# A feed-forward planner that knows the port, the transfer queue and the measured durations, and three more seven-product steps

## The chip, the cores and the metric

The kernel runs on one core of a Trainium2 chip. The core has a matrix engine (TensorE, PE in the profile), a vector engine (VectorE, DVE), a scalar engine (ScalarE, ACT), GpSimd (POOL) and a queue for transfers (SyncE, SP). The engines run side by side, each takes its own instructions in a fixed order, and they wait for each other by semaphores. The time is the device time of one execution in microseconds (us), lower is better. A difference of about 0.5% is what a measurement of this kernel can tell from no change.

## The reference

Two branches over the same 2048 rows `x` of width 576 are mixed by a gate. Branch A is linear attention with 32 heads of 18 columns. Branch B is a layer norm, a matrix `w1` to 4608 columns, a GELU, and a matrix `w2` back to 576 columns.

```python
def _A_ref(x, wqkv, wo):
    q, k, v = ...                                  # x @ wqkv, 32 heads of 18
    phi = lambda t: jnp.where(t > 0, t + 1, jnp.exp(t)) + 1e-6
    pq, pk = phi(q), phi(k)
    kv = jnp.einsum("bhsd,bhse->bhde", pk, v)
    z = jnp.einsum("bhsd->bhd", pk)
    num = jnp.einsum("bhqd,bhde->bhqe", pq, kv)
    den = jnp.einsum("bhqd,bhd->bhq", pq, z)[..., None] + 1e-6
    o = num / den                                  # the heads side by side again
    return o @ wo

def _B_ref(x, w1, b1, w2, b2):
    y = _layernorm(x, axis=-1)
    h = _gelu(jnp.einsum("bsd,df->bsf", y, w1) + b1)
    return jnp.einsum("bsf,fd->bsd", h, w2) + b2

g = _sigmoid((x * gate_w).sum(-1, keepdims=True))
return g * a + (1 - g) * b
...
```

## The kernel before

Branch A, the gate and the layer norm's sums fill the first 275 us, branch B's feed-forward the rest. This text is about the feed-forward, which begins where the tiles `wa`, `wb`, `h` and `region` appear.

**Numbers in two halves.** Every float32 factor is split into a high part (a copy into the type fp32r, made by ScalarE) and a low part (what is left, a subtraction by VectorE), and a product is taken as high x high, high x low and low x high. The tiles in the order listings are: `u` (the hidden values in float32), `h` (their two parts), `fresh` (raw `w1` and `w2` as they land, and sums of them), `wa` and `wb` (the split `w1`), `region` (the split `w2`), `accs` (the sums of the result in SBUF, and in its spare part the rows of `y`), `ystage` (split pieces of `y` on their way to memory), `ps` (PSUM, where the matmuls write).

**Steps.** The 4608 hidden columns are cut into 18 chunks of 256, the 2048 rows into two halves of 1024. A step `k` is one chunk for one half of the rows: steps 0 to 17 are the first half, 18 to 35 the second. In each step the `w1` product is made by Strassen's scheme in its Winograd form, two blocks by two blocks, with seven products (`up_product`) of seven 512-column matmuls each. The `w2` product of a step is made in the step after it, in one of two ways (`make_units`):

- plain: 8 units of 12 matmuls of 288 columns, 96 in all (`plain_unit`). Of the 8 evictions, those in `SEEDS` start from the running sum, which ScalarE copies into PSUM and back out; the others are added by VectorE (`accs<-ps,accs`).
- seven products: 14 units of 6 matmuls, 84 in all (`one_of_seven`), if `k` is in `SEVEN` (line 64). It needs four sums of blocks of `h` (`make_sum`, S1, S3, S2, S4 in that order, each `u<-u` and then split into `h`), four sums of blocks of `w2` (`sum_w2`, on GpSimd, `fresh<-fresh 128x288`), and it makes 12 evictions on VectorE.

The first half has work that the second has not: the four sums of `w1` (`sum_w1`, on GpSimd, `fresh<-fresh 128x384`), its split (`wa`, `wb`) and store, and the making of the second half's `y`. Before the change, `SEVEN` holds the odd steps of the first half up to 15 and all of 17 to 34, 26 steps, and all sums of `h` stand on GpSimd (`SUM_ENGINE`, line 74).

**The order.** No instruction of the feed-forward stands where the code lists it. `op` and `dma` record each operation with what it needs and gives; `nominal` gives due times by the matmuls' order; then a list planner (`choose`, `commit`) walks all engines by `COST`, a price for each engine as (fixed, per column, extra until the result is seen), and writes each engine's instructions in the order found. `port=True` marks operations with two inputs in SBUF: `when_` (line 1404) lets such an operation of VectorE or GpSimd begin, in the plan, from 135 ns before the end of the other engine's last such operation. Buffers (`h` 9, `u` 5, `w2` 7 places) are handed out by the plan too.

## Time and profile before

| what | value |
|---|---|
| median of 3 runs | 1116.88 us (1116.56 to 1120.96) |
| profiled execution, own time | 1116.29 us |
| its span, first to last instruction | 1114.6 us |
| granted TensorE clock over the span | 1.000 |
| PE / DVE / ACT / POOL busy, share of the span | 99% / 80% / 58% / 36% |

A row of busy time tells how long an engine had something in it. Matmuls overlap, and an end of one is modelled, so that a PE of 99% may still lose time; it is better read by how many matmuls of each width fall into a stretch. The table by stage (`us from the span's start`) cuts the span at 275 us, where the feed-forward begins, at 700 us, about where the second half of the rows begins, and at 1075 us, ahead of the end.

### The profile page before, as it was taken

What the parts mean: (1) busy time and instruction counts of PE and PEld (TensorE: products, weight loads), DVE (VectorE), ACT (ScalarE), POOL (GpSimd) and SP (SyncE); (2) the same over time, 40 slices, a digit from 0 to 9 for tenths busy, and PEclk for the clock granted to TensorE, in tenths of its full rate; (3) what the DMA queues carried; (4) which work ended last, traced back from release to release, by engine and by line L of the source; (5) the groups of instructions that cost most, each with busy time, mean ns of one, the idle gap of its engine ahead of it and who ended that gap; (6) DMA issues with size and microseconds to landing.
All of it is one profiled execution on the core that took longest, in us unless ns stands there. A gap on an engine that the chain in (4) does not pass through costs nothing.

```text
span 1114.6 us, 18587 instructions
## 1 busy us (share of the span) xinstructions
PE 1102.9 (99%) x6766; PEld 1004.2 (90%) x6766; DVE 890.6 (80%) x1381; ACT 647.6 (58%) x1158; POOL 398.2 (36%) x326
## 2 busy tenths in 40 slices
PE   9999999999999999999999999999999999999998
PEld 8999999999888898897898988889989899988998
DVE  4568784895887979879979997888887788778888
ACT  6677774443657566666756766355554555455542
POOL 2111112531335153533515543325444444344430
PEclk9999999999999999999999999999999999999999
DMA  6465762835635646463564649774445444544432
GB/s 183 125 89 184 171 227 102 316 118 210 220 124 181 203 153 233 158 240 129 185 221 157 223 145 380 273 249 122 128 119 147 128 118 127 143 126 125 121 110 86
DMA packets 108862, 189.42 MB, mean 170 GB/s; under 512 B 8924, under 2 KB 68588, under 8 KB 104674
## 3 DMA queue, kind: packets, MB, share of 16 engines
q1 hardware_dynamic: 107858, 187.49, 52.9%
q8 instruction: 53, 0.87, 0.3%
q10 hardware_dynamic: 720, 0.74, 0.2%
q14 instruction: 39, 0.32, 0.1%
q0 software_dynamic: 192, 0.01, 0.0%
HBM read 121.40 MB, written 66.80 MB: 169 GB/s over the span
## 4 chain that ended last, share of the span: by engine, by line
PE 77%; DVE 11%; DMA 5%; ACT 2%; issue 2%; SPq 2%; POOL 1%; ACTq 0%; DVEq 0%; POOLq 0%
PE ps L111 77%; DVE accs L111 3%; DVE h L111 2%; DVE region L111 2%; SPq L111 2%; DMA w1d<-wb 1%; DMA fresh<-in_ue 1%; DVE wb L111 1%; ACT u L111 1%; DVE wa L111 1%; DMA yd<-ystage 1%; DMA accs<-in_xe 1%; DVE u L111 1%; ACT h L111 1%; POOL u L111 0%
## 5 line engine op out<-in xcount | busy, mean ns | idle before, releaser
L111 PEld LDWEIGHTS ps<-region,h 128*128 128x128 f32 x3144 | 454.6, 188 | 43.8 <-DVE accs L111 6.9
L111 PE MATMUL ps<-region,h 128*128 128x288 f32 x3144 | 479.4, 295 | 5.4 <-ACT ps L111 2.0
L111 DVE TENSOR_TENSOR accs<-ps,accs 128x576 f32<-128x576 f32 x336 | 250.7, 754 | 87.8 <-PE ps L111 83.2
L111 POOL TENSOR_TENSOR fresh<-fresh 128x288 f32<-128x288 f32 (+1 forms) x164 | 173.7, 1067 | 372.3 <-DMA fresh<-in_w 281.0
L111 PE MATMUL ps<-y,wa 128*128 128x512 f32 x1008 | 269.0, 393 | 0.4 <-DVE wa L111 0.4
L111 PE MATMUL ps<-y,wb 128*128 128x512 f32 x756 | 203.8, 396 | 0.3 <-ACT u L111 0.3
L111 PEld LDWEIGHTS ps<-y,wa 128*128 128x128 f32 x1008 | 176.6, 188 | 25.6 <-DVE wa L111 1.3
L111 POOL TENSOR_TENSOR u<-u 128x512 f32<-128x512 f32 x104 | 163.7, 1574 | 96.8 <-DVE h L111 60.2
L111 DVE TENSOR_TENSOR h<-u,h 128x512 fp32r<-128x512 f32 x222 | 185.2, 849 | 5.4 <-ACT u L111 4.8
L111 PEld LDWEIGHTS ps<-y,wb 128*128 128x128 f32 x756 | 132.6, 188 | 23.3 <-ACT u L111 0.7
L111 ACT ACTIVATE u<-ps 128x512 f32<-128x512 f32 x73 | 43.7, 598 | 144.8 <-PE ps L111 144.8
L111 PE MATMUL ps<-y 128*128 128x288 f32 (+1 forms) x896 | 126.1, 297 | 1.1 <-ACT y L111 0.5
L111 PEld LDWEIGHTS ps<-y 128*128 128x128 f32 x896 | 122.4, 188 | 3.4 <-ACT y L111 1.3
L111 DVE TENSOR_TENSOR region<-fresh,region 128x576 fp32r<-128x576 f32 x120 | 99.5, 829 | 2.1 <-ACT region L111 1.7
L111 ACT ACTIVATE region<-fresh 128x576 fp32r<-128x576 f32 x120 | 74.1, 630 | 36.5 <-PE ps L111 32.1
L111 ACT ACTIVATE h<-ps,b1s 128x512 fp32r<-128x512 f32 x45 | 30.9, 686 | 77.4 <-PE ps L111 77.2
L111 ACT ACTIVATE h<-u,b1s 128x512 fp32r<-128x512 f32 x73 | 52.7, 721 | 32.1 <-DVE u L111 31.3
L111 ACT ACTIVATE h<-u 128x512 fp32r<-128x512 f32 x104 | 60.3, 621 | 17.3 <-POOL u L111 17.2
L111 DVE TENSOR_TENSOR wa<-fresh,wa 128x512 fp32r<-128x512 f32 x64 | 49.3, 770 | 19.2 <-ACT wa L111 13.8
L111 PE MATMUL ps<-wp,qt 128*128 128x288 f32 x448 | 63.3, 298 | 0.0
L111 DVE TENSOR_TENSOR u<-ps,u 128x512 f32<-128x512 f32 x74 | 50.9, 689 | 13.8 <-ACT u L111 11.7
L111 POOL TENSOR_TENSOR pks<-pks,k 128x576 f32<-128x576 f32 x15 | 21.9, 1459 | 108.7 <-DVE k L111 108.7
(122 smaller groups left out, 1037.9 us busy)
## 6 DMA issues: line engine op xcount, KB each, us to landing
w1d<-wa SPq DMA_DIRECT2D x17, 1280.0 KB
wa<-w1d SPq DMA_DIRECT2D x68, 320.0 KB
fresh<-in_w SPq DMA_DIRECT2D x70, 288.0 KB
y<-yd SPq DMA_DIRECT2D x14, 1280.0 KB
w1d<-wb SPq DMA_DIRECT2D x17, 960.0 KB
wb<-w1d SPq DMA_DIRECT2D x51, 320.0 KB
yd<-ystage SPq DMA_DIRECT2D x28, 320.0 KB
fresh<-in_um SPq DMA_DIRECT2D x64, 128.0 KB
```

Source lines behind the costliest of these rows:

```text
L111: return lambda *args, **kwargs: self.tc.keep_in_program_order(op(*args, **kwargs))
```

## The change

The numbers and names that are new:

- `SEVEN` has 29 steps: 1, 3, 6, 8, 9, 10, 11, 13 to 34. In the first half 11 of the steps 0 to 16 go by seven products (8 before).
- The sums of `h` are divided by `DVE_SUMS`: S1, S3 and S4 of the first half and S1, S3 and S2 of the second stand on VectorE, the others on GpSimd.
- `SEEDS` has three entries for four.
- The planner's prices of VectorE and ScalarE move by 1 ns; GpSimd's go from 30 + 2.5 per column to 250 + 2.19 per column. In the plan, an operation of GpSimd that uses the port begins 78 ns after VectorE's last such operation has ended (before: up to 135 ns ahead of its end), and `in_the_way` puts back an operation whose port time would run into one of the other engine that is due.
- Transfers are planned with their number of issues, a time for what they move, one after another, and no more than eight under way.
- Each GpSimd operation that uses the port gets a semaphore wait for the VectorE operation with the port that stands ahead of it in the plan, if that ended less than 4 us before (`add_manual_dep`).
- `plan` runs first and is written out after; its weights stand in `TUNED`, with an offset to the due time for each kind of operation.
- The last two of eight tiles of attention results for the end (`attn`) lie in `ystage`, not in `fresh`.

```diff
-SEVEN = {*range(1, NCHUNK - 1, 2), *range(NCHUNK - 1, LAST)}
-SEEDS = ((0, 0, 0), (0, 1, 0), (1, 0, 0), (1, 1, 0))
-SUM_ENGINE = {S1: "POOL", S3: "POOL", S2: "POOL", S4: "POOL"}
+SEVEN = set([1, 3, 6, 8, 9, 10, 11, 13, 14, 15, 16, 17, 18, 19, 20, 21, 22, 23, 24, 25, 26, 27, 28, 29, 30, 31, 32, 33, 34])
+DVE_SUMS = set([(2, False), (3, False), (3, True), (4, False), (4, True), (6, True)])
+SEEDS = ((0, 0, 1), (0, 1, 0), (1, 1, 0))
...
-    COST = {ACT: (90, 0.838, 97), DVE: (65, 1.0425, 83), POOL: (30, 2.5, -40)}
+    COST = {ACT: (91, 0.838, 97), DVE: (66, 1.0425, 84), POOL: (250, 2.19, -78)}
...
-        engine = SUM_ENGINE[m]
+        engine = DVE if (m, k < NCHUNK) in DVE_SUMS else POOL
...
-        if o.port:
-            other = POOL if o.engine == DVE else DVE
-            s = max(s, port_until[other] - 135)
...
+            if o.port:
+                s = max(s, port_until[POOL] - 135 if o.engine == DVE else port_until[DVE] + 78)
+            return s
+
+        def in_the_way(o, s):
+            other = POOL if o.engine == DVE else DVE
+            until = min(due[o], s + o.tail - 135 - shift - guard)
+            for u in port_line[other][port_at[other]:]:
+                if due[u] >= until:
+                    return False
+                if u not in done and due[u] + shift > s - 1500 and (missing[u] or ready[u] < s + o.tail - 135):
+                    return True
+            return False
...
+            if e == DMA:
+                service = (o.tail - o.ns - 1800) / o.issues
+                for n in range(o.issues):
+                    if len(landed) >= 8:
+                        s = max(s, landed[-8])
+                    s += o.ns / o.issues
+                    moved = max(moved, s + 600) + service
+                    t = moved + 1200
+                    landed.append(t)
...
+    end, sequence = plan(*TUNED)
+    before = None
+    for o, got, s, t in sequence:
+        for name, key, n in got:
+            places[name, key] = n
         o.f()
+        if o.port and o.engine == DVE:
+            before = dve.last.ins.name, t
+        if o.port and o.engine == POOL and before and before[1] > s - 4000:
+            tc.add_manual_dep(pool.last.ins, before[0], mybir.DependencyInfo(
+                mybir.DependencyClass.Sync, mybir.DependencyReason.DATA), reason="order")
```

Over the whole program the rows of the order count 36 matmuls `ps<-region,h` fewer (of 3140 shown), on DVE 87 sums `u<-u 128x512`, 29 evictions `accs<-ps,accs`, 9 low parts of `h` and 6 of `region` more, on POOL 75 sums `u<-u` fewer and 12 sums of `w2` more, on ACT 34 copies for the seeds fewer and, net, 21 of other kinds more. SP has 613 rows in both. Up to the feed-forward the rows of PE are the same.

On GpSimd, in step 9 (a seven-product step in both kernels), the sums of `w2` and of `h` and those of the next `w1` stood before as follows.

```order
L111 TENSOR_TENSOR fresh<-fresh 128x288 [waits DMAHW7_49,DMAHW6_49]
L111 TENSOR_TENSOR fresh<-fresh 128x288 [waits DVE_49,Activation_49,Pool_49]
L111 TENSOR_TENSOR fresh<-fresh 128x288 [waits Pool_49] x2
L111 TENSOR_TENSOR u<-u 128x512 [waits DVE_49,Activation_49]
L111 TENSOR_TENSOR u<-u 128x512 [waits Activation_49,Pool_49]
L111 TENSOR_TENSOR fresh<-fresh 128x384
L111 TENSOR_TENSOR u<-u 128x512 [waits DVE_49,Pool_49] x2
```

On the same engine, in step 9 of the changed kernel:

```order
L113 TENSOR_TENSOR fresh<-fresh 128x384 [waits DMAHW2_49,DMAHW1_49,DMAHW3_49,DMAHW0_49,DVE_49]
L113 TENSOR_TENSOR fresh<-fresh 128x384 [waits DMAHW4_49,DMAHW5_49,DVE_49,Pool_49]
L113 TENSOR_TENSOR fresh<-fresh 128x384 [waits DVE_49]
L113 TENSOR_TENSOR fresh<-fresh 128x384 [waits DMAHW6_49,DMAHW7_49,DVE_49,Pool_49]
L113 TENSOR_TENSOR fresh<-fresh 128x288 [waits DMAHW6_49,DMAHW5_49,Activation_49]
L113 TENSOR_TENSOR fresh<-fresh 128x288 [waits DVE_49,Pool_49]
L113 TENSOR_TENSOR fresh<-fresh 128x288 [waits Pool_49]
L113 TENSOR_TENSOR fresh<-fresh 128x288 [waits DVE_49,Pool_49]
L113 TENSOR_TENSOR u<-u 128x512 [waits DVE_49,Activation_49]
```

Of the step's four sums of `h` one is left on GpSimd, behind the sums of `w1` and `w2`, and nearly every instruction waits for one of VectorE, also where it needs nothing from it.

On VectorE, the same step before, where the low parts of `h` and `region` and the evictions alternate:

```order
L111 TENSOR_TENSOR accs<-ps,accs 128x2x288 [waits PE_49]
L111 TENSOR_TENSOR region<-fresh,region 128x2x288 [waits DMAHW7_49,DMAHW6_49,Activation_49]
L111 TENSOR_TENSOR u<-ps,u 128x512 [waits PE_49]
L111 TENSOR_TENSOR h<-u,h 128x512
L111 TENSOR_TENSOR h<-u,h 128x512 [waits Activation_49]
L111 TENSOR_TENSOR region<-fresh,region 128x2x288 [waits DVE_49,Pool_49]
L111 TENSOR_TENSOR accs<-ps,accs 128x2x288 [waits PE_49]
L111 TENSOR_TENSOR h<-u,h 128x512 [waits Activation_49,Pool_49]
L111 TENSOR_TENSOR h<-u,h 128x512 [waits Pool_49]
L111 TENSOR_TENSOR region<-fresh,region 128x2x288 [waits DVE_49,Activation_49]
```

And the same step on VectorE after the change:

```order
L113 TENSOR_TENSOR u<-u 128x512
L113 TENSOR_TENSOR accs<-ps,accs 128x2x288 [waits PE_49]
L113 TENSOR_TENSOR accs<-ps,accs 128x2x288
L113 TENSOR_TENSOR region<-fresh,region 128x2x288 [waits Activation_49]
L113 TENSOR_TENSOR h<-u,h 128x512 [waits Activation_49]
L113 TENSOR_TENSOR region<-fresh,region 128x2x288
L113 TENSOR_TENSOR u<-u 128x512 [waits DVE_49,Pool_49]
L113 TENSOR_TENSOR h<-u,h 128x512 [waits Activation_49] x3
L113 TENSOR_TENSOR accs<-ps,accs 128x2x288 [waits PE_49,Activation_49]
L113 TENSOR_TENSOR accs<-ps,accs 128x2x288 [waits PE_49]
```

Two sums `u<-u` stand among the low parts, and the evictions stand in pairs or longer runs.

More of the change, by code (lines that the diff above doesn't have):

```diff
@@ L887, in op @@
             tail = ns + c
-        o = Op(engine, f, ns, tail, needs, gives, port, take, give, by)
-        o.early = early
+        o = Op(engine, f, ns, tail, needs, gives, port, take, give, by, early, issues)
         ops.append(o)
@@ L1089, in there @@
             def there(keys=keys):
[L1090 removed]
+                at = [places["w2", key] for key in keys]
                 if len(at) > 1 and at[0] > at[-1]:
@@ L1109, in start_of @@
     def start_of(k, to, half, first):
-        if k % NCHUNK == 0 and first:
+        if k in (0, NCHUNK) and first:
             return b2b[:, None, half_cols(half)].to_broadcast([P, 2, HALF])
@@ new lines, in tile_gated_mix, with plan, offer, give @@
+    count = {o: sum(key in makers for key in o.needs) for o in ops}
+    in_order, left = [o for o in ops if not count[o]], dict(count)
+    for o in in_order:
+        for u in followers[o]:
+            left[u] -= 1
+            if not left[u]:
+                in_order.append(u)
+    assert len(in_order) == len(ops)
+    def plan(lag, late, slop, slack, guard, ahead):
+        slot, due = {o: n for n, o in enumerate(ups)}, {}
+        for o in downs:
+            _, k, j, n = o.by
+            slot[o] = (k + 1) * SLOTS + lag + j * SLOTS / n
+        t = 0.0
+        for o in sorted(ups + downs, key=lambda o: (slot[o], o.by[0] == "up")):
+            due[o] = t
+            t += o.ns
+        nominal = {o: due[o] for o in due}
+        for o in reversed(in_order):
+            out = [due[u] - o.tail - HEAR.get(u.engine, 0) for u in followers[o]]
+            if o in due:
+                out.append(due[o])
+            due[o] = min(out, default=1e9) - o.early - ahead.get(o.kind, 0)
+        missing, ready = dict(count), {o: 0.0 for o in ops}
+        line = {name: sorted(own, key=lambda o: due[o]) for name, own in lines.items()}
+        at = {name: 0 for name in lines}
+        room = {name: [(0.0, n) for n in range(size)] for name, size in ROOMS.items()}
+        room_of, done, sequence = {}, set(), []
+        free, port_until = {e: 0.0 for e in (PE, ACT, DVE, POOL, DMA)}, {DVE: -1e9, POOL: -1e9}
+        pending = {e: [] for e in free}
+        port_line = {e: sorted((o for o in ops if o.engine == e and o.port), key=lambda o: due[o]) for e in port_until}
+        port_at, moved, landed = {e: 0 for e in port_until}, 0.0, []
+        next_up, next_down, shift = 0, 0, 0.0
+        def offer(o):
+            if o.engine is None:
+                give(o, ready[o])
+            else:
+                pending[o.engine].append(o)
+        def give(o, t):
+            for u in followers[o]:
+                ready[u] = max(ready[u], t + HEAR.get(u.engine, 0))
```

334 lines of the change are left out of this document (143 added, 191 removed).

## The prediction, made before the changed kernel was run

> **What bounds the kernel now.** I read the page's busy shares first, then the table by stage, the waits of the matrix engine, and the timeline around its longest wait.
>
> ```profile
> span 1114.6 us, 18587 instructions
> PE 1102.9 (99%) x6766; PEld 1004.2 (90%) x6766; DVE 890.6 (80%) x1381; ACT 647.6 (58%) x1158; POOL 398.2 (36%) x326
> ```
>
> PE is busy all the time, so what shortens the kernel is fewer matmuls or fewer holes between them. How many holes there are is told by the table by stage, first for all instructions, then for those that touch `region` (on PE, the 288-column matmuls of the `w2` product; the busy columns are then PE, PEld, DVE and ACT alone), and by two rows of PE's timeline.
>
> ```profile
> core 0: us, PE busy (x) PEld busy (x) DVE busy (x) ACT busy (x) POOL busy (x), PEclk, DMA share, GB/s
> 275.00:700.00 425.00, 419.07 (x2464) 373.26 (x2463) 361.94 (x520) 270.16 (x441) 171.84 (x137) 1.00 0.58 199
> 700.00:1075.00 375.00, 375.00 (x2207) 336.71 (x2206) 301.26 (x417) 197.74 (x327) 161.24 (x130) 1.00 0.49 145
> ...
> 275.00:700.00 425.00, 235.39 (x1561) 222.87 (x1562) 51.30 (x54) 32.91 (x54) 1.00 0.58 199
> 700.00:1075.00 375.00, 216.59 (x1394) 205.31 (x1394) 44.70 (x61) 38.72 (x62) 1.00 0.49 145
> ```
>
> ```profile
> 820.61 1.76 PE L111 MATMUL ps<-region,h 128*128 128x288 f32 x12
> 822.20 1.09 PE L111 MATMUL ps<-y,wb 128*128 128x512 f32 x4
> ```
>
> Twelve 288-column matmuls take 822.20 - 820.61 = 1.59 us to the next start, 132.5 ns each. In the second half 1394 of them are 184.7 us; the other 2207 - 1394 = 813 (512 columns) share the 190.3 us left, 234.1 ns each. At this pace the first half's 1561 and 903 would be 206.8 + 211.4 = 418.2 us. They took 425. So the first half has 6.8 us of holes beyond what the second half has, and the clock is 1.00 in both. The waits of PE in the first half say whom it waits for:
>
> ```profile
> PE ps L111 <- ACT ps L111: 2.0, 3, 1.3
> PE ps L111 <- DVE accs L111: 2.0, 5, 0.5
> PE ps L111 <- DVE h L111: 1.0, 2, 0.7
> PE ps L111 <- DVE wa L111: 0.4, 1, 0.4
> PE ps L111 <- ACT u L111: 0.3, 1, 0.3
> ```
>
> The longest is the one of 1.27 us at 506 us, in a seven-product step. GpSimd's, VectorE's and PE's rows ahead of it:
>
> ```profile
> 497.11 3.07 POOL L111 TENSOR_TENSOR u<-u 128x512 f32<-128x512 f32 x2
> 501.58 3.50 POOL L111 TENSOR_TENSOR u<-u 128x512 f32<-128x512 f32 x2
> 505.05 1.44 POOL L111 TENSOR_TENSOR fresh<-fresh 128x384 f32<-128x384 f32 x1
> ```
>
> ```profile
> 497.27 1.76 DVE L111 TENSOR_TENSOR region<-fresh,region 128x576 fp32r<-128x576 f32 x1 [0.89 <-ACT region L111]
> 499.55 1.18 DVE L111 TENSOR_TENSOR h<-u,h 128x512 fp32r<-128x512 f32 x1
> 501.18 0.98 DVE L111 TENSOR_TENSOR h<-u,h 128x512 fp32r<-128x512 f32 x1 [0.45 <-ACT u L111]
> 502.09 1.84 DVE L111 TENSOR_TENSOR region<-fresh,region 128x576 fp32r<-128x576 f32 x1
> 503.85 0.74 DVE L111 TENSOR_TENSOR accs<-ps,accs 128x576 f32<-128x576 f32 x1
> 504.60 2.43 DVE L111 TENSOR_TENSOR h<-u,h 128x512 fp32r<-128x512 f32 x2
> ...
> 506.18 1.85 PE L111 MATMUL ps<-region,h 128*128 128x288 f32 x12 [1.27 <-ACT ps L111]
> ```
>
> While GpSimd sums, VectorE's operations with two inputs in SBUF last 1.0 to 1.8 us; the eviction, which has one input in PSUM, keeps its 0.74. The page's groups for the first half, the durations of single kinds over the feed-forward, and four rows of VectorE at 803 us give the undisturbed prices:
>
> ```profile
> L111 DVE TENSOR_TENSOR h<-u,h 128x512 fp32r<-128x512 f32 x99 | 82.6, 852 | 4.9 <-ACT u L111 4.8
> L111 DVE TENSOR_TENSOR region<-fresh,region 128x576 fp32r<-128x576 f32 x45 | 47.2, 1050 | 2.0 <-ACT region L111 1.7
> L111 DVE TENSOR_TENSOR wa<-fresh,wa 128x512 fp32r<-128x512 f32 x32 | 30.8, 962 | 18.3 <-ACT wa L111 13.8 <-DMA fresh<-in_ue 4.5
> L111 DVE TENSOR_TENSOR wa<-fresh,wa 64x256 fp32r<-64x256 f32 x32 | 18.5, 577 | 0.9
> L111 DVE TENSOR_TENSOR wb<-fresh,wb 128x768 fp32r<-128x768 f32 x16 | 15.2, 951 | 0.1
> ...
> L111 DVE TENSOR_TENSOR h<-u,h x221: 674/683/1780, 286.6 to 1099.4; 128x512 fp32r<-128x512 f32 x111
> L111 DVE TENSOR_TENSOR accs<-accs x32: 550/948/1770, 304.1 to 630.5; 128x768 f32<-128x768 f32 x16, 128x384 f32<-128x384 f32 x16
> L111 DVE TENSOR_TENSOR wa<-accs,wa x4: 422/554/693, 280.1 to 284.2; 128x512 fp32r<-128x512 f32 x2, 64x256 fp32r<-64x256 f32 x2
> ...
> 803.01 0.76 DVE L111 TENSOR_TENSOR accs<-ps,accs 128x576 f32<-128x576 f32 x1
> 803.69 0.68 DVE L111 TENSOR_TENSOR h<-u,h 128x512 fp32r<-128x512 f32 x1
> 804.29 0.75 DVE L111 TENSOR_TENSOR region<-fresh,region 128x576 fp32r<-128x576 f32 x1
> 804.96 0.75 DVE L111 TENSOR_TENSOR accs<-ps,accs 128x576 f32<-128x576 f32 x1
> ```
>
> An operation begins some 0.08 us before the last one's end is shown, so that the price on a full VectorE is the distance of starts: eviction 0.68, low part of `h` 0.60, of `region` 0.67. Against the undisturbed durations (0.68, 0.75, 0.69, 0.42) the first four groups lost 99 x 0.17 + 45 x 0.30 + 32 x 0.27 + 32 x 0.155 = 44 us to waiting for the port.
>
> **The change part by part.**
>
> *Fewer matmuls.* Three steps more by seven products: 3 x (96 - 84) = 36 matmuls x 132.5 ns = 4.8 us off PE. PE is the bound, so all of it counts.
>
> *The holes.* The change moves sums off GpSimd, plans GpSimd's port time at its measured length and makes it wait for VectorE. That aims at the holes of the kind at 506 us: behind ACT `ps`, DVE `accs` and DVE `wa`, 2.0 + 2.0 + 0.4 = 4.4 us. DVE `h` and ACT `u` (1.3 us) I leave: they are late by their own chain. Ends: nothing is gained (0) and all 6.8 us go. I take 4.4.
>
> *VectorE's new work.* A sum on VectorE is in no row. `accs<-accs`, also float32 and from SBUF alone, takes 550 ns for 384 columns and 948 for 768, so 512 lie near 683, or 0.60 from start to start, as `h<-u,h` does. Ends: 0.47 and 0.87 (384 and 768 columns, less 0.08); I take 0.60. Of the 87 sums 11 x 3 = 33 fall into the first half (20 us) and 18 x 3 = 54 into the second (32 us). The 29 evictions (x 0.68), 9 low parts of `h` (x 0.60) and 6 of `region` add 28 us in the first half. A seven-product step of the first half then asks of VectorE 12 x 0.68 + 7 x 0.60 + 3 x 0.60 + (3 x 0.67 + 0.36) for `region` + 3.25 for `wa` and `wb` (2 x 0.61, 2 x 0.34, 0.87, and 0.48 for the 64 rows of `wb`, between 256 and 512 columns) + 2 x 0.60 for `u<-ps,u` = 21.0 us. PE needs 49 x 0.2341 + 84 x 0.1325 = 22.6 us for it. Before, such a step (19.2 us, no sums) alternated with a plain one (10.9 us in 24.2 of PE). Now steps 8 to 11 and 13 to 16 run eight dense ones. Their cover is 1.6 us a step; it is gone when port waits exceed that. The making of `y` lies in the plain steps. In the planned order the POOL work (4 + 4 + 1 operations) stands beside evictions, as the rows of step 9 show, so I charge little: between 0 and the rivals' 9 us or more, I take 1.0 us, nearest to the second half, where VectorE with 54 sums is at 21.0 - 3.25 = 17.8 of 22.6 us and I charge nothing.
>
> *GpSimd's waits.* Behind a waiting instruction stand the sums of `w1` and `w2`, for which ACT's copies into `wa`, `wb` and `region` wait, and PE behind these. POOL is busy 171.84 of 425 us, so lateness has room: 0, at the other end the rivals' price.
>
> *ACT and transfers.* ACT loses 34 seed copies and gains 21 instructions net, at 270 of 425 us busy: 0. SP has as many issues; the `y` loads and attention tiles change places around 700 us, with a DMA share of 0.58 in that half. 0, within 2 us either way.
>
> *Sum,* against the profiled execution's own 1116.3 us: - 4.8 - 4.4 + 1.0 = 1108.1. The median of the runs stands 0.6 above that execution, inside what this forecast can tell; I say 1108.
>
> **A page's rule weighed.** VectorE shows 361.94 busy of 425 us in the first half while POOL shows 171.84. The Trainium skill, Perfetto Trace Analysis, Optimizing Scalar/DVE Operations, says that work of a saturated VectorE may be moved to ScalarE or even GpSimd, and adds that GpSimd and VectorE share a read port, so that moving between these two might not help. The change goes the other way. By the rule's first part the 33 sums of the first half cost 20 us uncovered (1116.3 - 4.8 + 20 = 1131); by its second part little is lost, and the 44 us of port waits side with the second. The time of the first part is that of the slower rival below.
>
> **The rivals.**
>
> *The port waits stay at their mean rate.* 44 us of waits on 171.84 us of POOL is 0.26 per us. POOL's first-half rows:
>
> ```profile
> L111 POOL TENSOR_TENSOR fresh<-fresh 128x384 f32<-128x384 f32 x64 | 79.2, 1250 | 207.4 <-DMA fresh<-in_w 145.2 <-DMA fresh<-in_ue 40.5 <-DMA yd<-ystage 10.6
> L111 POOL TENSOR_TENSOR u<-u 128x512 f32<-128x512 f32 x36 | 56.4, 1566 | 14.1 <-DVE accs L111 5.9 <-DVE h L111 4.2 <-ACT u L111 2.6
> L111 POOL TENSOR_TENSOR fresh<-fresh 128x288 f32<-128x288 f32 x36 | 37.5, 1041 | 25.3 <-ACT u L111 23.4
> ```
>
> A dense step has 4 x 1.25 + 4 x 1.04 + 1.57 = 10.7 us of POOL, 2.8 us of waits: 23.8 against 22.6, 1.2 x 8 = 9 us. With the 4.4 us won elsewhere 1116; with nothing won 1120.5. For it: the waits now are spread over all kinds. Against: sums on POOL and its unplanned length made many of them.
>
> *The holes only move.* The matmuls go, the holes stay or come back elsewhere: 1116.3 - 4.8 = 1111.5, up to 1115. For it: VectorE has more to do in the same time. Then most of what the change says of the order does nothing.
>
> *VectorE becomes the bound, slower.* In the ten us before 506 the waits were 1.01 + 0.50 + 0.30 + 1.09 + 1.15 = 4.05 us. If each dense step met that, it would take 25.0 us of VectorE, 2.4 x 8 = 19 us more: 1116.3 - 4.8 + 19 = 1130.5. It is slower than before by 0.5% from 2.9 us of waits a step (1.6 of cover, and 10.4 / 8).
>
> **How the numbers follow.** Forecast, 1103.5 (all 6.8 us and a little won) to 1111: 0.57. Waits at the mean rate 0.14, holes that move 0.12: both within 0.5% (1111.3 to 1122.5), which is about what a measurement can tell from no change. Bound by VectorE 0.17. So faster 0.57, same 0.26, slower 0.17. The range 1103 to 1120 leaves out the slower case and a small remainder; the likeliest case's own is 1103.5 to 1111.
>
> **What would show it.** 36 fewer 288-column matmuls. In the first half PE's waits for ACT `ps` and DVE `accs` near or under 1 us. The mean of `h<-u,h` near 0.70 for 0.85 and of `region` near 0.80 for 1.05. A sum `u<-u` on VectorE near 0.68 us. Wrong it would be if, between the middle of the first half and its end, a dense step takes over 23 us, with PE waiting for DVE `accs` or `h`, or if `wa` and `wb` come late behind GpSimd's waits.

## The result, and the profile after

The changed kernel takes 1107.81 us (median of 4 runs, 1106.87 to 1108.32) against 1118.21 us for the kernel before in the same comparison (4 runs, 1116.56 to 1120.96): a ratio of 0.990, 95% interval 0.988 to 0.993. The profiled execution has an own time of 1106.87 us and a span of 1105.2, 9.4 us less than the span of before; the granted clock is 1.00 in both.

The head of the page of the changed kernel, with the busy time and the instructions of each engine:

```profile
span 1105.2 us, 18592 instructions
PE 1097.0 (99%) x6730; PEld 1000.5 (91%) x6730; DVE 923.9 (84%) x1512; ACT 639.5 (58%) x1145; POOL 259.6 (23%) x263
```

PE has the 36 matmuls less (6766 before). VectorE (DVE) works 33 us more and GpSimd (POOL) 139 us less. The table by stage of the changed kernel follows, for all instructions and then for those that touch `region` (columns as in the prediction):

```profile
275.00:700.00 425.00, 422.60 (x2474) 376.09 (x2473) 392.02 (x609) 268.81 (x435) 122.09 (x124) 1.00 0.60 207
700.00:1075.00 375.00, 375.00 (x2216) 338.08 (x2216) 314.39 (x472) 196.62 (x330) 75.66 (x81) 1.00 0.46 138
...
275.00:700.00 425.00, 235.49 (x1555) 222.15 (x1556) 44.12 (x60) 36.33 (x60) 1.00 0.60 207
700.00:1075.00 375.00, 214.83 (x1400) 204.65 (x1400) 48.21 (x64) 39.49 (x64) 1.00 0.46 138
```

The same 425 us of the first half now hold 10 matmuls more than before (2474 for 2464), with 89 more instructions of DVE (609 for 520), which is now busy 392 of the 425 us. The same 375 us of the second half hold 9 more. PE's waits in the first half:

```profile
PE ps L113 <- ACT ps L113: 1.0, 1, 1.0
PE ps L113 <- DVE accs L113: 0.8, 3, 0.4
```

The rows for DVE `wa`, DVE `h` and ACT `u` are gone; 5.7 us of waits have become 1.8. Groups of the first half that use the port GpSimd and VectorE share, each form for itself, on VectorE and on GpSimd:

```profile
L113 DVE TENSOR_TENSOR h<-u,h 128x512 fp32r<-128x512 f32 x109 | 75.6, 711 | 0.9 <-ACT u L113 0.5
L113 DVE TENSOR_TENSOR region<-fresh,region 128x576 fp32r<-128x576 f32 x48 | 38.8, 809 | 0.5 <-ACT region L113 0.4
L113 DVE TENSOR_TENSOR wa<-fresh,wa 128x512 fp32r<-128x512 f32 x32 | 27.6, 864 | 13.5 <-ACT wa L113 13.4
...
L113 DVE TENSOR_TENSOR u<-u 128x512 f32<-128x512 f32 x36 | 26.5, 736 | 0.4
...
L113 DVE TENSOR_TENSOR wa<-fresh,wa 64x256 fp32r<-64x256 f32 x32 | 14.1, 444 | 0.7
...
L113 POOL TENSOR_TENSOR fresh<-fresh 128x384 f32<-128x384 f32 x64 | 65.5, 1037 | 186.8 <-DVE h L113 50.9 <-DVE accs L113 39.1 <-ACT ystage L113 20.7
L113 POOL TENSOR_TENSOR fresh<-fresh 128x288 f32<-128x288 f32 x48 | 40.1, 835 | 60.5 <-DMA fresh<-in_w 16.8 <-DVE h L113 15.9 <-DVE u L113 7.7
L113 POOL TENSOR_TENSOR u<-u 128x512 f32<-128x512 f32 x12 | 16.8, 1398 | 39.3 <-DVE u L113 21.6 <-DVE accs L113 13.1 <-DVE wb L113 4.0
```

Before the sums of `w1`, GpSimd's idle time was ended by transfers; now VectorE ends at least 50.9 + 39.1 of 186.8 us of it, which is what the added waits are for. Its sums are shorter (1250 to 1037 ns, 1041 to 835); the run without the waits below shows that they are so because they meet VectorE less at the port. Against the undisturbed durations of the prediction (0.68 us, 0.75, 0.69, 0.68, 0.42) the five groups of VectorE lose 3.4 + 2.8 + 5.6 + 2.0 + 0.8 = 14.6 us to the port, 44 before (there without sums). By the busy time of POOL that is 0.12 us per us, 0.26 before.

Where did the 9.4 us come from? I add up, over PE's matmuls, what lies between the starts of two neighbours beyond 132 ns (288 columns) or 231 ns (512 columns), distances that are shorter counting against it, and call the sum holes. It holds every loss of pace, also matmuls at a lower granted clock. The column "fewer matmuls" is against before.

| | fewer matmuls | holes 275 to 700 us | holes 700 to 1075 us |
|---|---|---|---|
| before | 0 | 10.8 | 3.6 |
| after | 36 x 132.5 ns = 4.8 us | 7.8 | 1.9 |

4.8 + 3.0 + 1.6 (from the unrounded sums) = 9.4 us, which is the difference of the spans. (By this count before has 10.8 us of holes in its first half. The prediction's 6.8 was what the first half had beyond the pace of the second; so it left out what both halves have.)

### The profile page after: what moved, and what is told of

Read it like the earlier page. It is cut to its first block, busy times and chain, and to the rows that moved or that the text cites. A ratio compares the mean times of both kernels' runs of the same rounds, so it can differ in the third digit from the quotient of the medians.

```text
span 1105.2 us, 18592 instructions
## 1 busy us (share of the span) xinstructions
PE 1097.0 (99%) x6730; PEld 1000.5 (91%) x6730; DVE 923.9 (84%) x1512; ACT 639.5 (58%) x1145; POOL 259.6 (23%) x263
## 4 chain that ended last, share of the span: by engine, by line
PE 84%; DVE 11%; issue 2%; ACT 1%; DMA 1%; SPq 0%; POOL 0%; ACTq 0%; DVEq 0%
PE ps L113 84%; DVE accs L113 3%; DVE u L113 2%; DVE h L113 2%; DVE wa L113 1%; DVE wb L113 1%; DVE region L113 1%; DMA fresh<-in_w 1%; DMA s<-in_wm 0%; ACT u L113 0%; DVE wp L113 0%; DVE den L113 0%; ACT y L113 0%; SPq L113 0%; POOL u L113 0%
## 5 line engine op out<-in xcount | busy, mean ns | idle before, releaser
L113 PEld LDWEIGHTS ps<-region,h 128*128 128x128 f32 x3108 | 448.0, 188 | 39.7 <-DVE accs L113 7.1
L113 PE MATMUL ps<-region,h 128*128 128x288 f32 x3108 | 472.3, 295 | 2.5 <-ACT ps L113 1.0
L113 DVE TENSOR_TENSOR accs<-ps,accs 128x576 f32<-128x576 f32 x365 | 270.0, 750 | 40.5 <-PE ps L113 38.1
L113 POOL TENSOR_TENSOR fresh<-fresh 128x288 f32<-128x288 f32 (+1 forms) x176 | 158.9, 909 | 334.2 <-DMA fresh<-in_w 110.2
L113 DVE TENSOR_TENSOR h<-u,h 128x512 fp32r<-128x512 f32 x231 | 159.9, 709 | 18.0 <-ACT u L113 16.3
L113 POOL TENSOR_TENSOR u<-u 128x512 f32<-128x512 f32 x29 | 38.9, 1340 | 263.0 <-DVE region L113 132.7
L113 ACT ACTIVATE h<-u 128x512 fp32r<-128x512 f32 x116 | 68.6, 620 | 9.3 <-POOL u L113 7.9
L113 DVE TENSOR_TENSOR u<-ps,u 128x512 f32<-128x512 f32 x74 | 50.5, 684 | 23.9 <-PE ps L113 12.4
L113 DVE TENSOR_TENSOR u<-u 128x512 f32<-128x512 f32 x87 | 61.2, 704 | 0.4
L113 ACT ACTIVATE ps<-ps 128x576 f32<-128x576 f32 (+1 forms) x93 | 57.4, 617 | 6.1 <-PE ps L113 3.4
L113 PEld LDWEIGHTS ps<-wp,qt 128*128 128x128 f32 x448 | 59.9, 188 | 0.3 <-DVE qt L113 0.2
```

The costliest lines, as they stand in the source:

```text
L113: self.last = self.tc.keep_in_program_order(op(*args, **kwargs))
```

## The experiments

The runs stood in four comparisons, each with runs of before beside them (medians 1118.2, 1116.6, 1116.6 and 1117.5 us), so the same kernel moved by up to 1.6 us from one comparison to another, and a difference of that size between two of them tells little. Two kinds of edits have to be kept apart. Those on the waits or on one operation keep the order of the kernel that they start from. Those on the planner or on the choice of steps have the order planned again, on the changed kernel with `TUNED`, weights that were searched for it; they may not fit the new problem, and two runs at the end measure how much that is. No run gives the old planner weights that were searched for it.

### The old order with 29 steps

On the kernel before:

```diff
-SEVEN = {*range(1, NCHUNK - 1, 2), *range(NCHUNK - 1, LAST)}
+SEVEN = set([1, 3, 6, 8, 9, 10, 11, 13, 14, 15, 16, 17, 18, 19, 20, 21, 22, 23, 24, 25, 26, 27, 28, 29, 30, 31, 32, 33, 34])
```

> The kernel before with the 29 seven-product steps alone, all sums on GpSimd, old planner. 4.8 us of matmuls go. A dense step then has 4 x 1.25 + 4 x 1.04 + 4 x 1.57 = 15.4 us of GpSimd at 0.26 us of port wait each, 4.0 us, on 19.2 us of VectorE: 23.2 against 22.6 us of the matrix engine, 0.6 x 8 = 5 us of new holes: 1116.5 us, between 1113 and 1121. If the planner and the place of the sums have no part in the gain, 1118.2 - 4.8 - 4.5 = 1108.9 us or less is not reached either, but 1113.4 is: nothing new opens.

1135.41 us, 1.017 of before (1.015 to 1.018), 18.8 us slower and far above the 1113 to 1121 that I expected. PE's longest waits of the first half (the first three rows), and the stage:

```profile
PE ps L111 <- DVE wa L111: 6.2, 5, 1.9
PE ps L111 <- DVE accs L111: 4.0, 13, 0.9
PE ps L111 <- DVE wb L111: 2.5, 6, 0.5
...
275.00:700.00 425.00, 407.08 (x2326) 353.06 (x2325) 382.52 (x537) 259.47 (x421) 192.44 (x153) 1.00 0.56 192
```

The 36 matmuls go here too, and 22.0 us of holes more come in the first half (32.8). The three longest waits are all for VectorE: it seems that three more steps at its old port waits (`h` at a mean of 839 ns) are more than it can do in this order. This is the slower rival of the prediction, in the kernel that keeps the old planner.

### The new planner with 26 steps

On the changed kernel, only `SEVEN` as it was before, the order planned again:

```diff
-SEVEN = set([1, 3, 6, 8, 9, 10, 11, 13, 14, 15, 16, 17, 18, 19, 20, 21, 22, 23, 24, 25, 26, 27, 28, 29, 30, 31, 32, 33, 34])
+SEVEN = {*range(1, NCHUNK - 1, 2), *range(NCHUNK - 1, LAST)}
```

> The changed kernel with the 26 seven-product steps of before. If the gain is made of two separate parts (36 matmuls at 132.5 ns are 4.8 us, closed holes about 4.5 us), the holes stay closed and only the matmuls come back: 1107.8 + 4.8 = 1112.6 us, down to 1111.5 if the dense steps 8 to 11 and 13 to 16 had holes of their own. If the weights of the plan fit only the 29 steps they stand beside, the new order opens holes: 1115 us or more. The mean of the low parts of h on VectorE stays near 0.71 us in the first half by both.

1115.20 us, 0.998 (0.997 to 0.9996). Taken alone it says that all but the steps gives 1.4 us and the three steps 7.4, more than their matmuls. That reading falls with the run on fitted weights below.

### The waits taken away, the order kept

```diff
-        if o.port and o.engine == POOL and before and before[1] > s - 4000:
+        if False:
             tc.add_manual_dep(pool.last.ins, before[0], mybir.DependencyInfo(
                 mybir.DependencyClass.Sync, mybir.DependencyReason.DATA), reason="order")
```

> The changed kernel in the same order on every engine, without GpSimd's added waits for VectorE. If these waits keep GpSimd from taking the port ahead of time, the low parts of h and region in the first half go from 0.71 and 0.81 us towards 0.85 and 1.05, and holes come back: 1109 to 1112 us. If the order and the fewer sums on GpSimd suffice, 1107.8 us within 0.7, and the durations stay.

1129.25 us, 1.012 (1.010 to 1.014): 21.4 us more than the changed kernel, where 1109 to 1112 was expected, with the same instructions on each engine in the same order. Stage, PE's waits, and the two groups that meet at the port:

```profile
275.00:700.00 425.00, 406.32 (x2342) 357.25 (x2341) 393.93 (x580) 256.96 (x415) 142.66 (x119) 1.00 0.54 185
...
PE ps L113 <- DVE accs L113: 11.6, 13, 1.7
PE ps L113 <- ACT ps L113: 3.4, 6, 0.9
PE ps L113 <- DVE h L113: 2.3, 3, 1.4
```

```profile
L113 DVE TENSOR_TENSOR h<-u,h 128x512 fp32r<-128x512 f32 x103 | 81.3, 808 | 1.0 <-ACT u L113 0.5
...
L113 POOL TENSOR_TENSOR fresh<-fresh 128x384 f32<-128x384 f32 x64 | 82.7, 1311 | 146.5 <-DMA fresh<-in_ue 64.5 <-DMA w1d<-wb 33.5 <-DVE accs L113 30.0
```

GpSimd mostly starts as soon as its transfer is there, so its sums run into VectorE's operations: its own last 1311 ns for 1037, and `h` 808 for 711. VectorE is busy about as long as with the waits (393.93 us for 392.02) but has done 29 instructions fewer by 700 us. Taken one by one, the 609 operations that VectorE does in the first half of the changed kernel last 23.8 us longer here in sum, while its idle time before them stays (39.8 and 39.4 us). PE waits for it behind `accs`. All of the loss is in the first half: 29.6 us of holes for 7.8, and 2.0 for 1.9 in the second, where VectorE is busy 314 of 375 us.

The Trainium skill, SBUF — State Buffer, "Who interferes with whom", says that a VectorE instruction with two inputs in SBUF contends with a GpSimd instruction that reads SBUF, and that issue order, not the shape of the operation, decides who blocks. This run agrees with it: it changes nothing but who comes first, and the durations of both engines change.

### The waits alone, on the old order

The recording of the last VectorE operation and the `add_manual_dep` as in the changed kernel, put into the kernel before:

```diff
+        if o.port and e == DVE:
+            port_before[0] = dve.last.ins.name, s + o.tail
+        if o.port and e == POOL and port_before[0] and port_before[0][1] > s - 4000:
+            tc.add_manual_dep(pool.last.ins, port_before[0][0], mybir.DependencyInfo(
+                mybir.DependencyClass.Sync, mybir.DependencyReason.DATA), reason="order")
```

> The kernel before (26 steps, all sums on GpSimd, old planner) with one part of the change alone: each GpSimd operation with the port waits for the VectorE operation ahead of it in the plan. If these waits close the holes, the 4.4 us behind ACT ps, DVE accs and DVE wa go: 1112 us. If they help only an order that was planned for them, GpSimd, which has 15 us of work in a seven-product step, gets late and PE waits for it: 1117 us or more.

1123.56 us, 1.0065 (1.0047 to 1.0083), 7.0 us slower than before. PE's longest wait and GpSimd's sums of `h` in the first half:

```profile
PE ps L113 <- ACT ps L113: 7.0, 9, 1.7
```

```profile
L113 POOL TENSOR_TENSOR u<-u 128x512 f32<-128x512 f32 x36 | 52.5, 1459 | 17.5 <-DVE h L113 12.4 <-DVE region L113 3.6 <-DVE wa L113 0.5
```

The sums wait 12.4 us for `h` of VectorE (4.2 before), and what needs them comes late. At the two longest waits of PE (1.7 us each, at 509 and 606 us) ScalarE has stood 2.3 us for a sum before its split, and the `ps` that PE waits for comes behind that. PE's waits for ACT `ps` were 2.0 us before and are 7.0 now. So the waits are no gain by themselves: they fix an order, and this one was not planned with them.

### All sums on GpSimd

```diff
-DVE_SUMS = set([(2, False), (3, False), (3, True), (4, False), (4, True), (6, True)])
+DVE_SUMS = set()
```

> The changed kernel with all four sums of h on GpSimd again, planned anew, 29 steps. VectorE loses 1.8 us a dense step (21.0 to 19.2), GpSimd gains three sums of about 1.35 us. If the planner's knowledge of the port closes the holes, wherever the sums stand, 1107 to 1109.5 us. If the move of the sums closes them, they come back with the port waits: 1112 us or more, low parts of h near 0.85 us in the first half.

1122.06 us, 1.005 (1.004 to 1.007), with PE waiting 5.2 us for DVE `h`. The order was planned with weights of another case here too; the fitted run is below.

### GpSimd's old price in the planner

```diff
-    COST = {ACT: (91, 0.838, 97), DVE: (66, 1.0425, 84), POOL: (250, 2.19, -78)}
+    COST = {ACT: (91, 0.838, 97), DVE: (66, 1.0425, 84), POOL: (30, 2.5, -40)}
```

> The changed kernel, planned with GpSimd's old price (30 + 2.5 per column) but with its waits for VectorE and all else. If the measured durations are part of the gain, the sums of w2 (planned 750, measured 880 from start to start) come late and block VectorE past the planned gap: low parts of h above 0.75 us in the first half, 1110 to 1114 us. If the added waits alone hold the order, 1107.8 us within 1.5.

1114.43 us, 0.998 (0.997 to 0.999): 6.6 us more than the changed kernel, 5.7 of them in the first half's holes (13.5). That is no more than what weights that don't fit cost in the two cases below (5.7 and 6.9 us), so what the right price is worth stays open.

### Seven products in every step

```diff
-SEVEN = set([1, 3, 6, 8, 9, 10, 11, 13, 14, 15, 16, 17, 18, 19, 20, 21, 22, 23, 24, 25, 26, 27, 28, 29, 30, 31, 32, 33, 34])
+SEVEN = set(range(1, 35))
```

> The changed kernel with all steps 1 to 34 by seven products, 34 for 29: 60 matmuls less, 8.0 us. If VectorE's 21.0 us (and about 0.5 more for the 64-row pieces) of 22.6 a step are the limit, the making of y (some 38 us) no longer finds plain steps to lie in: VectorE has 17 x 21.5 + 38 = 403 us and 1 us of port waits a step, 420 in all, against 384 us of the matrix engine, so some 30 us of new holes: 1130 us, between 1118 and 1140. If the planner finds room, 1100 to 1104 us.

1137.31 us, 1.018 (1.017 to 1.020). Stage, and PE's longest waits in the first half:

```profile
275.00:700.00 425.00, 403.44 (x2232) 345.99 (x2231) 403.57 (x635) 254.21 (x414) 137.02 (x145) 0.98 0.53 177
...
PE ps L113 <- DVE accs L113: 13.6, 17, 3.5
PE ps L113 <- DVE region L113: 3.2, 2, 2.6
```

Five steps more take 60 matmuls, 8.0 us, off PE and bring 37 us of holes in the first half (45.2), of which 6.9 us lie in 17.0 us that were granted half the clock (0.98 over the stage). VectorE is busy 403.57 of 425 us. With these weights its limit lies between 29 and 34 such steps, and past it the loss is steep, also if 6 to 7 us of it are weights that don't fit.

### The 64-row pieces done over 128 rows

In three places of each `w1` split, VectorE makes a low part for rows 64 to 127 alone. Here that operation covers all rows, with a factor for each row (0 for the upper 64, -1 for the lower), which leaves the upper rows with the values that they had. The order is that of the changed kernel.

```diff
+    low_half = keep.tile([P, 1], F32, name="low_half")
+    for n in range(2):
+        dve.memset(low_half[64 * n:64 * n + 64], -float(n))
...
-            dve.tensor_sub(w[64:P, :, 2], src[64:P, :, 2], raw(w[64:P, :, 2]))
+            dve.scalar_tensor_tensor(w[:, :, 2], raw(w[:, :, 2]), low_half[:, 0:1], src[:, :, 2], op0=OP.mult, op1=OP.add)
```

> The changed kernel in the same order, with the low part of w1's last 64 rows made over all 128 rows (times 0 or -1 for each row, added to the source), which gives the same values. In the changed kernel's dense step a 64-row operation begins 0.1 us later than others and lets the next begin only after its end: some 0.2 us for each of three a step. If VectorE's full steps make the holes left in the first half (about 6 us), 16 x 0.5 us of VectorE is won and 3 to 5 us of holes close: 1103 to 1105 us. If these holes have other causes, 1107.8 us within 1.

1103.23 us (1103.00 to 1103.60), 0.988 (0.986 to 0.990): 4.6 us faster than the changed kernel, with twice the rows in that operation. VectorE's timeline in one step of the changed kernel, from one split of `wb` to the next:

```profile
542.81 0.94 DVE L113 TENSOR_TENSOR wb<-fresh,wb 128x768 fp32r<-128x768 f32 x1
543.68 0.74 DVE L113 TENSOR_TENSOR region<-fresh,region 128x576 fp32r<-128x576 f32 x1
544.45 0.56 DVE L113 TENSOR_TENSOR wb<-fresh,wb 64x384 fp32r<-64x384 f32 x1
545.04 0.69 DVE L113 TENSOR_TENSOR u<-u 128x512 f32<-128x512 f32 x1
545.65 1.42 DVE L113 TENSOR_TENSOR accs<-ps,accs 128x576 f32<-128x576 f32 x2
...
555.82 1.55 DVE L113 TENSOR_TENSOR accs<-ps,accs 128x576 f32<-128x576 f32 x2 [0.53 <-PE ps L113]
557.29 1.13 DVE L113 TENSOR_TENSOR wa<-fresh,wa 128x512 fp32r<-128x512 f32 x2
558.45 0.69 DVE L113 TENSOR_TENSOR u<-ps,u 128x512 f32<-128x512 f32 x1
...
565.95 0.95 DVE L113 TENSOR_TENSOR wb<-fresh,wb 128x768 fp32r<-128x768 f32 x1
```

And the same step with the whole rows:

```profile
540.97 0.94 DVE L113 TENSOR_TENSOR wb<-fresh,wb 128x768 fp32r<-128x768 f32 x1
541.84 0.75 DVE L113 TENSOR_TENSOR region<-fresh,region 128x576 fp32r<-128x576 f32 x1
542.50 0.61 DVE L113 SCALAR_TENSOR_TENSOR wb<-wb,low_half,fresh 128x384 fp32r<-128x384 f32 x1
543.03 0.68 DVE L113 TENSOR_TENSOR u<-u 128x512 f32<-128x512 f32 x1
...
563.61 0.95 DVE L113 TENSOR_TENSOR wb<-fresh,wb 128x768 fp32r<-128x768 f32 x1
```

Between full-row operations the next one starts 0.07 to 0.09 us ahead of the last one's end, whichever kind of operation it is (540.97 + 0.94 = 541.91, the next at 541.84; 541.84 + 0.75 = 542.59, the next at 542.50). The 64-row piece starts only after the end of `region` (543.68 + 0.74 = 544.42, start 544.45), and what comes behind it only after its own end (544.45 + 0.56 = 545.01, start 545.04). From `region` to `u<-u` it is 1.36 us in the one and 1.19 in the other, though the full-row piece itself is longer. The step takes 565.95 - 542.81 = 23.1 us in the one and 563.61 - 540.97 = 22.6 in the other, and 22.6 is what PE needs by the prediction's sum. The first half's holes fall from 7.8 to 3.9 us, those of the second half stay (1.9); PE's waits:

```profile
PE ps L113 <- ACT ps L113: 0.7, 1, 0.7
PE ps L113 <- DVE accs L113: 0.3, 1, 0.3
```

The Trainium skill, VectorE: DVE Perf Modes, "Two Vector instructions with no wait between them", says that an instruction whose input starts in another group of 32 rows than that of the instruction before is held until every earlier one has finished. It names the start row, not the number of rows, and the rows agree: the piece starts at row 64, its neighbours at row 0, and both it and its successor are held. (The rows `wa` x2 have a full-row operation and its 64-row piece in one.) Whether a piece over rows 0 to 63 would go unheld was not run.

### Thirty steps on whole rows

The last kernel (e8), with a planner's price of 60 ns more for that operation, step 5 by seven products too, and the weights searched anew.

```diff
-SEVEN = set([1, 3, 6, 8, 9, 10, 11, 13, 14, 15, 16, 17, 18, 19, 20, 21, 22, 23, 24, 25, 26, 27, 28, 29, 30, 31, 32, 33, 34])
+SEVEN = set([1, 3, 5, 6, 8, 9, 10, 11, 13, 14, 15, 16, 17, 18, 19, 20, 21, 22, 23, 24, 25, 26, 27, 28, 29, 30, 31, 32, 33, 34])
...
-                gives=[group + (2,)], port=True)
+                gives=[group + (2,)], port=True, more=60)
```

> The 128-row form of the low parts (as in e8_whole_tails, 1103.2 us), with a price for it in the planner, one more seven-product step (step 5, 30 in all) and the planner's weights searched anew for that. My theory, that VectorE still has about 0.5 us to spare in a step with seven products once the 64-row pieces are gone: 1101 to 1103 (1.6 us of matmuls less than e8, the holes as there, 7 us). Rival, that 29 is already VectorE's limit in this form too: 1104 or more, with new waits of TensorE on accs of VectorE before 700 us.

1102.91 us (1102.62 to 1103.12), 0.987 (0.986 to 0.989). It is the fastest of all, but by 0.3 us, which is not told from e8. The holes did not stay as they were in e8, as my theory had it. The spans say where the step's 1.6 us went: 1101.4 for 1101.9, since the first half's holes rise from 3.9 to 4.9. VectorE is busy 399.62 of 425 us there. So the thirtieth step paid hardly anything.

### The planner without the queue of transfers

```diff
-                    if len(landed) >= 8:
-                        s = max(s, landed[-8])
                     s += o.ns / o.issues
-                    moved = max(moved, s + 600) + service
+                    moved = s + 600 + service
                     t = moved + 1200
```

> The changed kernel, replanned with transfers that land after their latency alone in the planner (no queue of transfers); the port and the waits of GpSimd's sums stay, and so do the weights. My theory, that the transfers' queue sets little of the order here: 1107 to 1110, where up to 3 us is what weights that were searched for another planner cost. Rival, that the queue in the plan is a main part of the gain: 1113 or more, with waits of TensorE or ScalarE for transfers that the changed kernel does not have.

1119.86 us, 1.002 (1.001 to 1.003): 12.1 us more than the changed kernel, as the rival has it. Its longest wait of PE, and what stands ahead of it on the other engines, by the timeline:

```profile
417.63 3.05 POOL L113 TENSOR_TENSOR fresh<-fresh 128x384 f32<-128x384 f32 x3 [11.64 <-DMA fresh<-in_ue]
420.50 0.52 ACT L113 ACTIVATE ystage<-accs 128x384 fp32r<-128x384 f32 x1 [4.06 <-DMA yd<-ystage]
422.24 0.57 ACT L113 ACTIVATE u<-ps 128x512 f32<-128x512 f32 x1
422.87 1.56 PE L113 MATMUL ps<-y,wb 128*128 128x512 f32 x3 [3.57 <-ACT u L113]
```

ScalarE stands 4.06 us behind a store of `ystage`, which this plan lets land after its latency alone; the copy of `u` out of PSUM stands behind that, and PE waits for it. From 423.0 us on, right behind this wait, half the clock is granted for 3.4 us, which holds another 1.4 us of holes. The changed kernel has one such wait of ScalarE for that transfer in the first half, by its row among the waits of ScalarE, and no wait of PE behind it:

```profile
ACT ystage L113 <- DMA yd<-ystage: 1.6, 1, 1.6
```

So the queue does matter at this place (3.6 us). How much of the other 8 is the queue, and how much weights that don't fit, is open.

### The 26 steps and the sums on GpSimd again, with weights searched for them

`TUNED` alone is changed against the two runs above, found by the kernel's own planner for the case.

```diff
-TUNED = (2.5, 5, 10, 1000, 600, {'sum': 300, 'w2raw': 6000, 'u3': 300, ...
+TUNED = (3, 5, 60, 1000, 300, {'sum': -700, 'w2raw': 300, 'u3': -300, ...
```

> The changed planner with the 26 seven-product steps of before, as e1_new_plan_26 (1115.2 us), but with the planner's weights searched anew for them. If part of e1's distance to before less the holes is weights that did not fit: 1111.5 to 1113. If the new order is worth only 1.4 us at 26 steps: 1115 again.

1109.53 us (1109.16 to 1109.78), 0.993 (0.992 to 0.995): below both expectations, 5.7 us less than with the weights of the 29 steps, and 1.7 us more than the changed kernel. PE's waits in the first half, as few as in the changed kernel but for one:

```profile
PE ps L113 <- ACT ps L113: 2.3, 2, 1.2
PE ps L113 <- DVE accs L113: 1.2, 3, 0.4
```

Its holes are 6.4 and 0.6 us. So with the same 26 steps as before, all the rest of the change together (planner, waits, place of the sums, seeds and searched weights) takes away 4.4 + 3.0 = 7.4 us of holes; the three steps then take 4.8 us off PE and give back 1.4 + 1.4. How much of the 7.4 us is what the planner now knows, and how much the search of its weights, no run tells, since the old planner was not searched for.

```diff
-TUNED = (2.5, 5, 10, 1000, 600, {'sum': 300, 'w2raw': 6000, 'u3': 300, ...
+TUNED = (2.5, 6, 10, 1000, 300, {'sum': 300, 'w2raw': 6000, 'u3': 1500, ...
```

> The changed planner with none of its sums on VectorE, as e4_sums_on_pool (1122.1 us), but with the planner's weights searched anew for that. If e4's loss of 14 us to the changed kernel was weights that did not fit: 1109 to 1113. If it is the place of the sums (longer ones on GpSimd, which now also wait for VectorE): 1118 or more, with TensorE waiting for h of VectorE.

1115.19 us, 0.998 (0.997 to 0.999): between the two expectations. Of the 14.3 us that the sums on GpSimd had cost, 6.9 were weights, and 7.4 are left to the place of the sums. The groups of the first half and, in the last row, of the second:

```profile
L113 DVE TENSOR_TENSOR h<-u,h 128x512 fp32r<-128x512 f32 x108 | 83.1, 783 | 2.4 <-ACT u L113 1.0 <-ACT h L113 0.7
...
L113 POOL TENSOR_TENSOR u<-u 128x512 f32<-128x512 f32 x48 | 65.4, 1362 | 84.3 <-DVE h L113 25.3 <-DVE accs L113 17.4 <-DVE region L113 16.0
...
L113 DVE TENSOR_TENSOR h<-u,h 128x512 fp32r<-128x512 f32 x114 | 89.2, 804 | 18.8 <-ACT u L113 18.8
```

A sum takes 1362 ns on GpSimd and 736 on VectorE in the changed kernel, and with the sums on GpSimd VectorE's `h` is longer (783 for 711 ns; 804 for 709 in the second half). Holes: 12.1 and 5.8 us for 7.8 and 1.9.

### All runs side by side

| kernel | order | steps | us | holes, first half | second |
|---|---|---|---|---|---|
| before | old | 26 | 1116.6 to 1118.2 | 10.8 | 3.6 |
| e7, waits alone | old | 26 | 1123.6 | 16.6 | 4.6 |
| e2 | old | 29 | 1135.4 | 32.8 | 4.5 |
| e11, weights searched | new | 26 | 1109.5 | 6.4 | 0.6 |
| e1, weights of the 29 | new | 26 | 1115.2 | 9.9 | 2.1 |
| after | new | 29 | 1107.8 | 7.8 | 1.9 |
| e3, without the waits | new | 29 | 1129.3 | 29.6 | 2.0 |
| e12, sums on GpSimd, weights searched | new | 29 | 1115.2 | 12.1 | 5.8 |
| e4, the same, weights of after | new | 29 | 1122.1 | 19.0 | 5.2 |
| e5, GpSimd's old price, weights of after | new | 29 | 1114.4 | 13.5 | 3.3 |
| e10, no queue, weights of after | new | 29 | 1119.9 | 18.6 | 4.5 |
| e8, whole rows | new | 29 | 1103.2 | 3.9 | 1.9 |
| e9, whole rows, weights searched | new | 30 | 1102.9 | 4.9 | 2.0 |
| e6, weights of after | new | 34 | 1137.3 | 45.2 | 3.2 |

In the profiled executions of e3, e4, e6 and e10 half the clock was granted for 3.4, 6.8, 17.0 and 3.4 us of the first half; the matmuls that start in these stretches hold 1.6, 2.4, 6.9 and 1.4 us of the holes in the table. What `SEEDS`, the attention tiles in `ystage` and `in_the_way` are worth by themselves was not run.

## Why the prediction was right, step by step

The predicted 1108 us was met (1107.8), but that they are so near each other is in part luck. On the profiled executions 1108.1 was forecast and 1106.87 measured, and the medians fell by 10.4 us: the kernel before had a median of 1118.2 beside the changed one, not the 1116.9 that the forecast started near. Of 8.2 us forecast and 9.4 measured, the matmuls gave the 4.8 that were forecast, the first half's holes 3.0 (4.4 - 1.0 = 3.4 forecast), and the second half's holes 1.6, for which nothing was forecast.

*Fewer matmuls,* -4.8 us: right as a count, x6766 to x6730, and it shows in full in the spans. As an account of what the three steps are worth it was too much: next to the order found for 26 steps they bring 1.7 us (2.1 by the spans), as 2.8 us of holes come back.

*The holes,* -4.4: right in the mechanism, as the run without the waits and the one with the sums on GpSimd show. Of the three waits that were to go (ACT `ps`, DVE `accs`, DVE `wa`) 2.6 of 4.4 us went. The two that I left (DVE `h` and ACT `u`, 1.3 us) as late by their own chain went too; the ones at 289 and 292 us stood behind a VectorE that met GpSimd's sums from 285.0 to 290.4 us, where a pair of `h` took 2.92 us and a `region` 1.57. With the 64-row pieces out of the way the first half loses 6.9 us of holes (10.8 to 3.9), near the upper end that I had set. Nothing was predicted for the second half, and 1.6 us went there. `h` has a mean of 709 ns for 849 (while `region` went from 824 to 857), by these two rows, before and then after, of the stretch from 700 to 1075 us. With the sums back on GpSimd it is 804 ns, and the holes of the second half are 5.8 us.

```profile
L111 DVE TENSOR_TENSOR h<-u,h 128x512 fp32r<-128x512 f32 x114 | 95.4, 849 | 0.5 <-ACT h L111 0.5
```

```profile
L113 DVE TENSOR_TENSOR h<-u,h 128x512 fp32r<-128x512 f32 x118 | 81.6, 709 | 17.1 <-ACT u L113 15.8 <-ACT h L113 1.3
```

I had taken the second half as free of holes because it has no listed waits of PE, and measured the first half against its pace.

*VectorE's new work,* +1.0: the term that was mis-sized. The sum on VectorE was right (0.60 from start to start; in the step shown above `u<-u` starts at 545.04 and the next at 545.65). The dense step was not 21.0 us of VectorE. I had priced the 64-row pieces at duration less overlap, 0.34 twice and 0.48; they cost 558.45 - 557.29 - 0.60 = 0.56 twice and 1.36 - 0.66 = 0.70. That makes 21.7 us and a cover of 0.9, not 1.6. The step shown took 23.1 us for 22.6 all the same, and not by port waits: but for the three pieces its operations last as long as in the kernel with whole rows, which needs 22.6. VectorE also waits for PE in this step (0.53 us ahead of 555.82), so its cover is not all free where it is needed. Of the 7.8 us of holes left in the first half, 3.9 hang on the pieces, which were in the kernel before as well. What the denser steps opened is told best by the run on 26 steps with searched weights: 1.4 us in the first half, and 1.4 in the second, for which I had charged nothing.

*GpSimd's waits,* 0: small in this order, but not nothing, and it hid the main thing. The one wait of PE for ACT `ps` that is left (1.0 us, at 597.55) stands behind a sum of `h` on GpSimd, which had waited 0.63 us for VectorE's `h` and took 1.75 us. The waits are not free and not neutral: without them the same order is 21.4 us slower, and on the old order they cost 7.0. The prediction named them as a part of *The holes* and did not price them.

*ACT and transfers,* 0 within 2 us: not contradicted; ScalarE is busy 268.81 us for 270.16, and the DMA share went from 0.58 to 0.60. That the queue in the plan has a part in the gain, the run without it shows at one place (3.6 us).

Of the rivals, *the port waits at their mean rate* did not come: 0.12 us per us of POOL, not 0.26. *The holes only move* did not come either, though 2.8 us of them did come back with the three steps. *VectorE becomes the bound* was a real one: the kernel without the waits takes 1129.3 us, near its 1130.5, with PE behind DVE `accs` through port waits, as was named. The step that I showed takes 25.1 us there, the rival's 25.0. Only about half of the loss lies in such dense steps, though; two steps with six evictions instead of twelve take 3.1 and 4.2 us more.

Moving sums onto a nearly full VectorE came out as I took it: with VectorE at 392 of 425 us the kernel is 7.4 us faster than with the sums on GpSimd at 170 of 425.

What was to show it: PE's waits for ACT `ps` and DVE `accs` at 1.0 and 0.8 (near or under 1), `h` 711 ns (0.70), `region` 809 (0.80), as foreseen; `u<-u` on VectorE 736 (0.68), and 681 in the second half, where GpSimd is busy 76 of 375 us. A dense step over 23 us, which was to be the sign of a wrong forecast, did come (23.1 us), at less than it was feared to cost.

## What to carry to other kernels

Where two engines share a port, plan their order and then bind it with waits. Here the waits on the old order made it 7.0 us slower, and the planned order without them was 21.4 us slower than with them. Price an instruction on a full engine from start to start in its own surroundings, since a duration does not show what an operation costs the ones beside it; operations that start at another row than their neighbours are worth looking for. When one part of a planned order is taken back to see its worth, tune the plan again first: here weights that did not fit cost 5.7 and 6.9 us, about as much as the parts that were to be measured.

## What the runs showed that I had not expected

- A 64-row operation of VectorE between full-row ones costs 0.17 us more than the same work over all 128 rows (1.36 and 1.19 us over the same two intervals), three times a step, 4.6 us of kernel time.
- With the same order and the same instructions, only GpSimd's start against VectorE's changed: a 384-column sum takes 1311 ns for 1037, a low part of `h` 808 for 711, and the kernel 21.4 us more.
- Seven products in all 34 steps, 8 us less of matmuls, are 29.5 us slower than in 29, or some 6 us (29.5 / 5) for each step more, where one below VectorE's limit gains at most 1.6. The weights of that run were those of the 29 steps and may have a part of 6 to 7 us in it, and half the clock, granted for 17.0 us, another 6.9.
